# Feeding two open sums one K tile at a time, with three other groups of work moved by one to three steps, in a fused hash-attention and SiLU feed-forward kernel

## The chip, the cores and the metric

The kernel runs on one core of a Trainium2 chip. The metric is device time in microseconds (us) of one execution. Every execution quoted here is with a granted TensorE clock of 0.999 or 1.0. Engine names are those of the profile: PE is TensorE (PEld its weight loads), DVE is VectorE, ACT is ScalarE, POOL is GpSimd, SP is SyncE.

## The reference

Attention over 4 batches x 8 heads with 768 positions and head dimension 64, in which a query sees only keys with the same 6-bit hash, and then a feed-forward layer on the result.

```python
def _attn_ref(q, k, v, proj):                     # cut
    q_bits = (einsum('bhsd,dk->bhsk', q, proj) > 0)
    k_bits = (einsum('bhsd,dk->bhsk', k, proj) > 0)
    ...                                           # buckets from the bits
    mask = q_bucket[:, :, :, None] == k_bucket[:, :, None, :]
    scores = where(mask, scale * matmul(q, k.transpose(0, 1, 3, 2)), -1e9)
    ...                                           # softmax
    return matmul(attn, v)

def _moe_ref(x, w_in, w_out):                     # x: 3072 x 512, w_in: 512 x 2048
    h = x @ w_in
    g = h * (1.0 / (1.0 + exp(-h)))
    return g @ w_out
```

## The kernel before

The attention of 32 heads is cut into 288 steps, nine to a head. A step `w` multiplies the probabilities of step `w` with V (four matmuls, line 398), and then issues the score of step `w + 3` (line 366), whose exponential (line 369) runs on ACT. All other work is planned into steps as filler: transposes of Q and K, the hash projection, and the feed-forward layer of the batch before.

```python
    LEAD = 3
    ...
    for w in range(NW):
        flush()                       # products g = (th + 1) * h of the step before, on DVE
        for fn in at.pop(w, []):      # work planned into this step
            fn()
        ...
        for _ in range(n):
            moeq.popleft()()          # units of the feed-forward layer
        av(w)
        if w + LEAD < NW:
            score(w + LEAD)
```

In the timelines shown here, an engine's instructions stand in the order in which the program issues them (in step 93 of the changed kernel the projection at 65.72 us, then line 398 at 67.15 and line 366 at 67.29). The feed-forward layer of batch 0 needs the output of all four pairs of heads as its four K tiles (`xT[0]` to `xT[3]`; a K tile is one quarter of the dimension that the sum runs over). The last one exists only after step 71. So two of its sums are opened before, with the first three tiles, and left open in PSUM, the memory in which PE adds up. They share the tag `m`, which has three buffers, with the transposes and the projections.

```python
        def mm1(ci, grp, dts=slice(0, NDT)):
            ...
            hp = opened.pop((ci, grp), None)
            if hp is None:
                hp = ps.tile([P, f, n], F32, tag="m", name="h_ps", bufs=3)
            for j in range(f):
                ft = grp * f + j
                for dt in range(dts.start, dts.stop):
                    nc.tensor.matmul(hp[:, j, :], w_in16[:, dt, ft * P : (ft + 1) * P],
                                     xT[4 * b + dt][:, c0 : c0 + n],
                                     start=(dt == 0), stop=(dt == NDT - 1))
            if dts.stop < NDT:
                opened[ci, grp] = hp
                return
            th = thp.tile([P, f, n], F32, tag="th", name="th")
            nc.scalar.activation(out=th, in_=hp, func=AF.Tanh, scale=0.5)
            after.append(lambda: nc.vector.scalar_tensor_tensor(...))     # g, line 470
```

The hash bits come from a projection on PE (line 281), a comparison on DVE (line 287), and copies into the operands of the scores. For pairs up to 7 these copies are DVE instructions (lines 340 and 343), eight for two pairs; for later pairs they are DMAs:

```python
        if p > 7:
            ...
            for n in range(2):
                nc.sync.dma_start(...)
            return
        for n in range(2):
            ...                       # tensor_copy or tensor_scalar on DVE
```

The softmax here doesn't subtract the row's maximum and nothing guards it: scores larger than these inputs give would overflow.

## Time and profile before

| | before |
|---|---|
| median of the first 3 executions | 304.34 us (304.14 to 304.92) |
| span of the profiled execution | 302.8 us |
| PE / ACT / DVE / POOL busy | 98% / 69% / 60% / 42% |
| chain that ended last | PE 91%, DVE 6%, ACT 1% |

How to read it: PE looks like the limit with 98%, and for the last three quarters of the span it is. The prediction shows the views of the first quarter, where other engines set the pace. Two more lines belong to it, from the timeline of PE. The columns are start and length in us, engine, line, operation, and in brackets the idle time of PE before it and what ended that.

```profile
66.66 1.02 PE L461 MATMUL h_ps<-xT,win 128*128 128x512 f16 x4 [0.62 <-DVE g L470]
...
74.50 1.02 PE L461 MATMUL h_ps<-xT,win 128*128 128x512 f16 x4 [0.21 <-DVE g L470]
```

These are the only two waits of PE on DVE in the whole span that the page counts (0.8 us). Both are for a PSUM buffer of tag `m` that a product of line 470 must free. The first stands right after the projection of pairs 6 and 7; the change is aimed at it.

### The profile page before, as it was taken

The page shows a single profiled execution, that of the slowest core. Times are in us where ns is not written, and L with a number is a line of the kernel's source. Part 1 is how long each engine was busy: PE and PEld are TensorE (multiplying, and loading weights), DVE is VectorE, ACT ScalarE, POOL GpSimd, SP SyncE. Part 2 cuts the span into 40 slices and gives each one's busy share as a digit, 9 for nine tenths or more (in the row PEclk, how much of TensorE's full clock was granted, in tenths as well). Part 3 has the DMA queues.
Part 4 walks back from the last instruction along what each step waited for, and adds up shares of the span by engine and source line. Part 5 has one row for each costly group of instructions (what it writes and reads, how often), then busy time and mean ns, then how long its engine had stood idle before and what let it go on. Part 6 is the DMA issues. An engine that isn't in the chain of part 4 may idle for free.

```text
span 302.8 us, 7181 instructions
## 1 busy us (share of the span) xinstructions
PE 297.2 (98%) x2710; PEld 175.1 (58%) x2710; DVE 180.3 (60%) x344; ACT 210.2 (69%) x392; POOL 128.3 (42%) x203
## 2 busy tenths in 40 slices
PE   8999999999999999999999999999999999999996
PEld 3675855545665665555565665555566654446653
DVE  5797848899668454854695434854543442764332
ACT  5987989979887686878886766878877732452300
POOL 7589999286617561845149411765111100000000
PEclk9999999999999999999999999999999999999999
DMA  7999997979988737844068226011022003001112
GB/s 195 246 251 196 187 164 123 244 124 163 160 180 137 116 106 194 132 92 134 3 125 131 62 61 202 1 42 31 2 61 63 6 32 95 35 2 69 37 66 73
DMA packets 103170, 32.87 MB, mean 109 GB/s; under 512 B 90656, under 2 KB 100192, under 8 KB 103136
## 3 DMA queue, kind: packets, MB, share of 16 engines
q1 hardware_dynamic: 98752, 28.22, 44.1%
q0 software_dynamic: 4224, 4.19, 9.0%
q8 instruction: 21, 0.34, 0.5%
q14 instruction: 13, 0.11, 0.1%
q10 hardware_dynamic: 160, 0.00, 0.0%
HBM read 27.27 MB, written 6.29 MB: 111 GB/s over the span
## 4 chain that ended last, share of the span: by engine, by line
PE 91%; DVE 6%; ACT 1%; issue 1%; POOL 0%; DVEq 0%; ACTq 0%; POOLq 0%
PE o_ps L496 26%; PE h_ps L461 24%; PE s_ps L366 19%; PE o_ps L398 12%; PE bp_ps L281 3%; DVE g L470 2%; PE tp_ps L185 2%; PE warm_ps L125 1%; PE o_ps L482 1%; ACT u L369 1%; DVE qk L246 1%; PE tp_ps L198 1%; DVE qka L343 1%; PE bp_ps L225 1%; PE o_ps L389 0%
## 5 line engine op out<-in xcount | busy, mean ns | idle before, releaser
L369 ACT ACTIVATE u<-s_ps 128x512 f16<-128x512 f32 x288 | 157.1, 602 | 37.7 <-PE s_ps L366 37.2
L470 DVE SCALAR_TENSOR_TENSOR g<-th,h_ps 128x512 f16<-128x512 f32 x96 | 65.7, 689 | 75.0 <-ACT th L468 75.0
L461 PE MATMUL h_ps<-xT,win 128*128 128x512 f16 (+1 forms) x512 | 97.7, 325 | 0.8 <-DVE g L470 0.8
L398 PEld LDWEIGHTS <-u 128*128 128x128 f16 x1152 | 68.1, 98 | 41.8 <-ACT u L369 8.2
L496 PE MATMUL o_ps<-wout,g 128*128 128x512 f16 x368 | 91.6, 379 | 0.0
L468 ACT ACTIVATE th<-h_ps 128x512 f32<-128x512 f32 x96 | 58.0, 604 | 38.0 <-PE h_ps L461 35.5
L398 PE MATMUL o_ps<-vv,u 128*128 128x65 f16 x1152 | 82.6, 194 | 0.7 <-ACT u L369 0.4
L461 PEld LDWEIGHTS <-win 128*128 128x128 f16 x512 | 49.8, 98 | 32.3 <-issue 1.6
L418 POOL TENSOR_TENSOR x_pr<-osum,rec 128x384 f16<-128x384 f32 x23 | 19.0, 826 | 89.7 <-DVE rec L417 89.2
L496 PEld LDWEIGHTS <-g 128*128 128x128 f16 x368 | 35.8, 98 | 33.6
L366 PE MATMUL s_ps<-qka 71*128 71x512 f16 x192 | 52.6, 327 | 0.1
L366 PE MATMUL s_ps<-qkb 128*128 128x512 f16 x192 | 52.5, 326 | 0.0
L251 POOL TENSOR_SCALAR qka<-qk 64x1536 f16<-64x1536 f32 x15 | 22.0, 1466 | 11.5 <-DVE qk L246 6.5
L501 DVE TENSOR_SCALAR osb<-o_ps 128x512 f32<-128x512 f32 x23 | 15.8, 688 | 15.0 <-PE o_ps L496 15.0
L251 POOL TENSOR_SCALAR qkb<-qk 64x1536 f16<-64x1536 f32 x15 | 22.1, 1471 | 1.2
L262 POOL TENSOR_TENSOR vsa<-v_sb 128x192 f32<-128x192 f32 x32 | 18.9, 592 | 0.0
L260 POOL CAST vv<-v_sb 128x384 f16<-128x384 f32 x32 | 16.2, 507 | 1.8 <-DMA v_sb<-in_v_dram 1.4
L246 DVE STREAM_TRANSPOSE qk<-k_blk 128x768 f32<-128x768 f32 x10 | 15.9, 1589 | 0.3 <-issue 0.3
L246 DVE STREAM_TRANSPOSE qk<-q_blk 128x768 f32<-128x768 f32 x10 | 15.9, 1594 | 0.0
L366 PEld LDWEIGHTS <-qka 71*128 71x128 f16 x192 | 15.5, 97 | 0.7 <-ACT qka L238 0.6
L366 PEld LDWEIGHTS <-qkb 128*128 128x128 f16 x192 | 15.4, 97 | 0.0
L412 DVE TENSOR_TENSOR osum<-o_ps,vsum 128x390 f32<-128x390 f32 x23 | 13.0, 565 | 2.3
(70 smaller groups left out, 162.9 us busy)
## 6 DMA issues: line engine op xcount, KB each, us to landing
out_dram<-osb SPq DMA_DIRECT2D x23, 256.0 KB
v_sb<-in_v_dram SPq DMA_DIRECT2D x15, 384.0 KB
q_blk<-in_q_dram SPq DMA_DIRECT2D x40, 96.0 KB
k_blk<-in_k_dram SPq DMA_DIRECT2D x40, 96.0 KB
win<-in_moe_w_in_dram POOLq DMA_DIRECT2D x4, 512.0 KB, 8.0
wout<-in_moe_w_out_dram POOLq DMA_DIRECT2D x4, 512.0 KB, 6.3
q_sb<-in_q_dram SPq DMA_DIRECT2D x5, 384.0 KB
k_sb<-in_k_dram SPq DMA_DIRECT2D x5, 384.0 KB
```

The source lines that it names most:

```text
L246: nc.vector.transpose(out=dst, in_=qk_sb[p, "qk"[n]])
L251: nc.gpsimd.tensor_scalar(out=dst[rows, :], in0=qk32[p][rows, :], scalar1=CS, scalar2=1.0, op0=ALU.mult, op1=ALU.mult)
L260: nc.gpsimd.tensor_copy(out=vv[:, :, 0:D], in_=src)
L262: nc.gpsimd.tensor_tensor(out=sa, in0=src[:, 0:3], in1=src[:, 3:6], op=ALU.add)
L366: nc.tensor.matmul(sp[:, o0 : o0 + n], t[rows, S + jt * P : S + (jt + 1) * P], t[rows, c0 : c0 + n], start=True, stop=True)
L369: nc.scalar.activation(out=u, in_=sp, func=AF.Exp, scale=ESC)
L398: nc.tensor.matmul(o_ps[h][:, c0 // P + i, :], u[:, o0 + i * P : o0 + (i + 1) * P], vv[:, jt, :], start=(not direct(h) and w % NU == 0 and ...
L418: (nc.vector if direct(h) else nc.gpsimd).tensor_tensor(out=x_pr[p][:, :, par * D : (par + 1) * D], in0=o[:, 0:NJ, 0:D], in1=rec[:, :, Non ...
L461: nc.tensor.matmul(hp[:, j, :], w_in16[:, dt, ft * P : (ft + 1) * P], xT[4 * b + dt][:, c0 : c0 + n], start=(dt == 0), stop=(dt == NDT - 1))
L468: nc.scalar.activation(out=th, in_=hp, func=AF.Tanh, scale=0.5)
L470: after.append(lambda: nc.vector.scalar_tensor_tensor(out=g[ci][:, grp * f : (grp + 1) * f, :], in0=th, scalar=1.0, in1=hp, op0=ALU.add, o ...
L496: nc.tensor.matmul(o2[tt], g[ci][:, ft, ct * P : (ct + 1) * P], w_out16[:, ft, :], start=(ft == 0), stop=(ft == NFT - 1))
```

## The change

The intent is to fill PE more evenly in the early part of the program and to take the projection away from the sum that follows it. Four things move and nothing is added or removed. The two open sums get one K tile at a time, at steps 65, 67, ... 75, where before they got three tiles each at steps 66 and 70. The transposes of head 7's output, which make the fourth tile, move from step 74 to 75. The transposes and casts of pairs 4 and 5 come three steps sooner. The projection of pairs 6 and 7 comes one step later.

```diff
             hp = opened.pop((ci, grp), None)
-            if hp is None:
+            if dts.start == 0:
                 hp = ps.tile([P, f, n], F32, tag="m", name="h_ps", bufs=3)
...
-            head = slice(0, NDT - 1)
-            first = [lambda grp=grp: mm1(0, grp, head) for grp in range(2)] + \
-                [lambda grp=grp: mm1(0, grp, slice(NDT - 1, NDT)) for grp in range(2)] + first[2:]
+            one = [[lambda grp=grp, dt=dt: mm1(0, grp, slice(dt, dt + 1)) for grp in range(2)]
+                   for dt in range(NDT)]
+            first = one[0] + one[1] + one[2] + one[3] + first[2:]
...
-        plan(QST + 3 * i, lambda i=i: t_unit(4 + i // 3, i % 3))
+        plan(QST - 3 + 3 * i, lambda i=i: t_unit(4 + i // 3, i % 3))
...
-                plan(QST + 3 * i, lambda p=4 + i // 3, par=par: cast_unit(p, par))
+                plan(QST - 3 + 3 * i, lambda p=4 + i // 3, par=par: cast_unit(p, par))
...
-        wp = w0 + (24 if Q == 2 else 20)
+        wp = w0 + {2: 24, 3: 21}.get(Q, 20)
...
-        plan((30, 42, 58)[p] if p < 3 else 2 * NU * (p + 1) + (2 if p % 4 == 3 else 9),
+        plan((30, 42, 58, 75)[p] if p < 4 else 2 * NU * (p + 1) + (2 if p % 4 == 3 else 9),
...
-    for i in range(2):
-        plan(66 + 4 * i, first_units[0].pop(0))
+    for i in range(6):
+        plan(65 + 2 * i, first_units[0].pop(0))
```

## The prediction

> **What bounds the kernel now.** I read the page's totals and chain first, then busy time by stretch, then the three engines' timelines in the stretches that the change touches.
>
> ```profile
> PE 91%; DVE 6%; ACT 1%; issue 1%; POOL 0%; DVEq 0%; ACTq 0%; POOLq 0%
> ...
> L369 ACT ACTIVATE u<-s_ps 128x512 f16<-128x512 f32 x288 | 157.1, 602 | 37.7 <-PE s_ps L366 37.2
> ...
> L461 PE MATMUL h_ps<-xT,win 128*128 128x512 f16 (+1 forms) x512 | 97.7, 325 | 0.8 <-DVE g L470 0.8
> ```
>
> The chain is almost all PE, and PE waits little. But a busy PE may still be slow, so I cut the span where the program changes character (columns: us, then busy us of PE, PE weight load, DVE, ACT, POOL).
>
> ```profile
> 44.40:56.00 11.60, 11.06 (x135) 6.43 (x132) 9.57 (x17) 10.64 (x22) 8.21 (x18) 1.00 0.87 172
> 56.00:74.50 18.50, 17.67 (x168) 9.66 (x166) 18.06 (x30) 16.11 (x33) 13.12 (x17) 1.00 1.00 154
> 74.50:245.00 170.50, 170.43 (x1629) 102.73 (x1629) 96.25 (x160) 130.82 (x243) 70.41 (x109) 1.00 0.45 93
> ```
>
> Three regimes follow one another: before 56 us ACT is nearly full, from 56 to 74.5 us DVE is (18.06 of 18.50), after that PE is without a gap. Everything the change moves lies before about 77 us. After 74.5 us PE runs its queue with no wait worth counting, so whatever PE gains up to there comes out at the end one for one, and nothing else does.
>
> To place the change I counted steps: every step of the main loop leaves one group of four probability-times-V matmuls (L398), and the score of three steps later follows it. Step 0's group starts at 9.07 us; step 36 is at 31.12, step 60 at 44.39, step 66 at 47.62, step 74 at 51.91, step 92 at 67.52.
>
> The ACT timeline of steps 63 to 80, with the idle time before a run of exponentials in brackets:
>
> ```profile
> 48.22 2.06 ACT L369 ACTIVATE u<-s_ps 128x512 f16<-128x512 f32 x4 [0.18 <-PE s_ps L366]
> 50.47 3.61 ACT L369 ACTIVATE u<-s_ps 128x512 f16<-128x512 f32 x7 [0.19 <-PE s_ps L366]
> 53.95 0.62 ACT L468 ACTIVATE th<-h_ps 128x512 f32<-128x512 f32 x1
> ```
>
> The two gaps are the two heads of the open sums (steps 66 and 70). Six exponentials take 3.04 us, so queued ones start (3.04 - 0.60)/5 = 0.49, or nearer 0.48, apart, less than their length of 0.60. A bare step costs PE 0.34 us (for example 47.62 to 47.96). Hence before step 80 a step lasts 0.48 us unless PE adds more than it can hide.
>
> The DVE timeline decides a second point, when the last attention output needed for batch 0 exists:
>
> ```profile
> 44.10 1.26 DVE L287 TENSOR_SCALAR bits<-bp_ps,sc 128x512 f16<-128x512 f32 x2 [1.16 <-PE bp_ps L281]
> ...
> 50.95 0.56 DVE L418 TENSOR_TENSOR x_pr<-o_ps,rec 128x384 f16<-128x384 f32 x1
> 52.11 0.56 DVE L431 COPY xT<-xt_ps 128x768 f16<-128x768 f16 x1 [0.60 <-PE xt_ps L430]
> ```
>
> From the bits of pairs 4 and 5 (44.10) to head 7's output (50.95 + 0.56 = 51.51) DVE never stops; PE's transposes of that output start at 51.56, right behind it.
>
> Last, pieces of the chain of waits in order of time:
>
> ```profile
> 55.55 0.50 ACT th L468
> 56.07 0.69 DVE g L470
> ...
> 66.04 0.57 DVE g L470
> 66.60 1.19 DVE bits L287 x2
> ...
> 73.76 0.70 DVE g L470
> 74.50 1.02 PE h_ps L461 x4
> ```
>
> It runs on DVE from 56.07, released by the second tanh of batch 0, to 74.50, where a PE sum waits for the buffer that this DVE result frees. In between PE loses 0.62 us at 66.66 and 0.21 us at 74.50, both waiting for L470 (all of the 0.8 in the page's row).
>
> **What the Trainium skill says.** "PSUM — Partial Sum Buffer", section "The four PSUM rules": a matmul without the first flag adds where an earlier one has written, and the clearing by a first one reaches its own bank. So a sum in its own bank may stay open while other banks are used; the kernel before already does this with three of four K tiles, and the change only splits it further. "TensorE: Matmul & The Clock Gate", section "Back-to-back issue gap": N/2.4 + 2.5 ns, 216 ns at N = 512; here the three head matmuls take PE 0.65 us (49.22 to 49.87), so the trace agrees, and splitting costs nothing extra (steps 77 and 79, which already carry one such matmul, take 0.56 = 0.34 + 0.22). "ScalarE: Activation LUTs", section "What ACT_TABLE_LOAD costs": 186 + 0.833 N ns, 612 at 512, with 93 ns overlapped; the trace has 602 and a spacing of about 480, so the overlap here is larger and I use the trace. "Perfetto Trace Analysis", section "Optimization Strategy", speaks of regimes with different limiting engines; the stretches above are a case.
>
> **The change part by part.** No work is added or removed; the same instructions are issued at other steps. I carry two start times from step to step, with constants from the trace: an exponential starts 0.48 after the one before it, or 0.60 after the PE group that its scores follow (47.62 to 48.22), whichever is later; a PE group starts 0.34 plus the extra PE work after the one before it, or 0.65 after its own exponential (39.87 to 40.52), whichever is later. A tanh takes a place of 0.48 in ACT's queue. Started at step 31 this account gives the kernel before within 0.2 us up to step 90, so I trust it for differences.
>
> *Transposes sooner.* Six units of 0.44 us (four transposes; 0.78 - 0.34 at step 39) go from steps 36..51 to 33..48. With one such unit every third step PE needs (3 x 0.34 + 0.44)/3 = 0.49 per step, as much as ACT. Moving the whole comb only exchanges an empty stretch before it for one after it. The account gives -0.06 us from step 54 on.
>
> *Sums fed one K tile at a time.* Before, steps 66 and 70 carry 0.65 us each: the exponentials of steps 69 and 73 start 0.82 and 0.80 after their forerunners instead of 0.48, a loss of 0.34 + 0.32 = 0.66. After, steps 65, 67, .. 75 carry 0.22 us each: two steps need 0.34 + 0.56 = 0.90 of PE against 0.96 of ACT, and the exponential three steps on has about 0.2 us to spare. So 0.63 to 0.66 is saved by step 73. But step 75 now has transposes (0.35) and a tile (0.22) together, and PE arrives there at about 51.26 us while head 7's output, at the end of the DVE run, exists only at 51.51 - 0.06 = 51.45. PE starts the transposes at about 51.50, group 75 at 51.50 + 0.35 + 0.22 = 52.07, the exponential of step 78 at 52.67 against 53.00 before. So about half is given back: -0.33 us, the shift of the projection's start included. The two tanh follow in ACT's queue, and the DVE run from 56.07 starts 0.33 sooner.
>
> *Projection one step later.* Before, step 92 has the projection (0.34 + 1.5 us with the step) and then a sum that wants the buffer of the sum just before; hence the wait of 0.62. After, that sum comes first and takes an older buffer, and step 93 had no sum, so the wait at 66.66 goes. But DVE does the same work in another order: L470 for that sum before the bits, and all eight copies of bits (steps 93 to 96) still before the L470 (flushed at step 97) on which PE waits at 74.50. DVE had no idle time there to recover. PE arrives 0.62 sooner and waits 0.62 longer. I give this part 0.0, at most 0.07 from two small gaps (DVE 0.10 at 74.69, PE 0.07 at 76.10), and put in 0.05.
>
> Sum: -0.33 - 0.05 = -0.38. 304.34 - 0.38 = 303.96.
>
> **The rivals.** (1) *Head 7's output does not hold PE up.* Then the account alone gives -0.56 at step 80, with the last 0.05 about 303.7. For it: PE's wait in the trace before is below 0.1. Against: DVE is continuous up to that output, and nothing in the change shortens that run. (2) *The removed 0.62 us wait reaches the end*: -0.33 - 0.62, or 303.4. For it: it is the longest wait of PE after 40 us. Against: DVE busy 18.06 of 18.50. (3) *Nothing arrives*: if DVE, not ACT, set its own start at 56 us, the time stays at 304.3. Against: DVE idles 0.78 us just before 56.07, waiting for the tanh. (4) *A new wait*: two open sums hold two of the three m buffers from step 67 instead of 70; only the step 75 transposes want the third, so I see no loss.
>
> **Range and chances.** The three runs before spread over 0.8 us. Rival 2 sets the low side, rival 3 with noise the high one: 303.3 to 304.5. 2% is 6 us. Steps 31 to 81 take 28.1 us (28.20 to 56.33), 50 x 0.34 of it bare steps and some 8.3 other PE work, which leaves 2.8 to win there and 0.8 after it; both outer chances are 0.01.
>
> **What would show it.** Right: the gaps of ACT before the exponentials of steps 69 and 73 are gone; a PE wait on L418's output of about 0.2 to 0.3 us appears before the L430 transposes of step 75; the first L470 of the long DVE run comes near 55.7; the wait of PE on L470 after the projection vanishes and the one now at 74.50 grows to 0.8 or 0.9. Wrong: that last wait stays near 0.2 (then rival 2), or the span falls by over 0.7 us, or by nothing.

## The result, and the profile after

The changed kernel took 304.39 us (median of 4, 303.95 to 304.45), the kernel before 304.38 us (median of 4) in the same rounds. The ratio of times was 0.9995, with a 95% interval of 0.9978 to 1.0012. A ratio here is the mean time of one kernel's fast runs over that of the other's of the same rounds, so it is not quite the ratio of the medians quoted. By the times alone, nothing can be seen.

The profiles show more, if they are laid over each other at the right point. The PE timeline of the first microseconds differs although both programs are the same there. Kernel before:

```profile
3.27 0.87 PE L198 MATMUL tp_ps<-ident,q_row 128*128 128x128 f32 x3
...
5.52 0.85 PE L225 MATMUL bp_ps<-qk,pw 128*32 128x384 f32 x8
...
9.07 0.30 PE L398 MATMUL o_ps<-vv,u 128*128 128x65 f16 x4
```

Changed kernel:

```profile
3.41 0.87 PE L198 MATMUL tp_ps<-ident,q_row 128*128 128x128 f32 x3
...
5.71 0.97 PE L225 MATMUL bp_ps<-qk,pw 128*32 128x384 f32 x8
...
9.38 0.30 PE L398 MATMUL o_ps<-vv,u 128*128 128x65 f16 x4
```

The first transposes began 0.14 us later here, and the first projection took 0.97 us where it took 0.85 (its successor began at 6.61 and not at 6.30), so step 0 began at 9.38 and not at 9.07 us. These 0.31 us stay in every start time that follows, and they cover up the gain of the change. To see that gain I use a distance: from the start of step 30's group of line 398 to the start of step 104's. Step 30 lies before everything that was moved (27.63 us before, 27.93 after), and step 104 after it (77.35 and 77.22). The distance is 49.72 us before and 49.29 us after: 0.43 us were won. From step 104 to step 287 both profiles take 167.77 us, so nothing is won or lost there.

The stretches of the changed kernel, with the columns of the prediction's view:

```profile
44.40:56.00 11.60, 11.20 (x139) 6.38 (x132) 9.79 (x17) 10.50 (x22) 8.55 (x19) 1.00 0.93 137
56.00:74.50 18.50, 17.66 (x169) 9.68 (x167) 18.08 (x30) 16.93 (x34) 13.12 (x17) 1.00 1.08 192
```

DVE is as full between 56 and 74.5 us as it was (18.08 for 18.06 us).

ACT's timeline of steps 65 to 78:

```profile
46.20 6.48 ACT L369 ACTIVATE u<-s_ps 128x512 f16<-128x512 f32 x13
52.96 0.60 ACT L369 ACTIVATE u<-s_ps 128x512 f16<-128x512 f32 x1 [0.27 <-PE s_ps L366]
```

Thirteen exponentials now run without a gap; the two gaps of 0.18 and 0.19 us are gone. But there is a new one of 0.27 us at 52.96. PE's timeline shows where it comes from:

```profile
51.27 0.30 PE L398 MATMUL o_ps<-vv,u 128*128 128x65 f16 x4
51.40 0.38 PE L366 MATMUL s_ps<-qka 71*128 71x512 f16 x1
51.80 0.51 PE L430 MATMUL xt_ps<-ident,x_pr 128*128 128x128 f16 x6
```

Two 512-column matmuls in sequence start 0.22 us apart elsewhere in this trace (52.14 and 52.36, for example). The transposes of line 430 could have started at 51.62 and started at 51.80: PE stood 0.18 us behind head 7's output, which DVE finished at 51.74. (No bracket appears there, since the modelled end of the score lies at 51.78.) The rest of the gap of 0.27 comes from the transposes and the tile in one step: in e7 below, where PE does not wait there, a gap of 0.08 us is left.

Further on, PE's timeline has one wait on DVE in place of two:

```profile
64.43 1.02 PE L461 MATMUL h_ps<-xT,win 128*128 128x512 f16 x4
...
65.72 1.50 PE L281 MATMUL bp_ps<-qk,pw 128*32 128x512 f32 x16
...
74.38 1.02 PE L461 MATMUL h_ps<-xT,win 128*128 128x512 f16 x4 [0.84 <-DVE g L470]
```

The sum now comes ahead of the projection and waits for nothing. The wait of 0.62 us is gone, and the wait that was 0.21 us at 74.50 is 0.84 at 74.38. Their sum was 0.83 and is 0.84. The bracket counts from the modelled end of the score before it. The expectations below count by the length of step 101, which is 1.58 us before, 2.21 in the changed kernel and 1.21 in e5, where PE does not wait: 0.37 and 1.00 us. By either count this wait grew by 0.63.

DVE's timeline of the changed kernel shows why. The sum at 74.38 needs the buffer of the last product here, which ends at 73.64 + 0.69 = 74.33, behind the copies of bits and without a gap of more than 0.03 us:

```profile
69.97 0.60 DVE L340 TENSOR_SCALAR qkb<-bits,sc 13x768 f16<-13x768 f16 x1
70.60 0.69 DVE L470 SCALAR_TENSOR_TENSOR g<-th,h_ps 128x512 f16<-128x512 f32 x1
71.32 1.10 DVE L343 COPY qka<-bits 13x768 f16<-13x768 f16 x2
72.44 0.54 DVE L343 COPY qkb<-bits 13x768 f16<-13x768 f16 x1
73.00 0.61 DVE L340 TENSOR_SCALAR qkb<-bits,sc 13x768 f16<-13x768 f16 x1
73.64 0.69 DVE L470 SCALAR_TENSOR_TENSOR g<-th,h_ps 128x512 f16<-128x512 f32 x1
```

The chain of the changed kernel shows 2% on a DMA of V, ahead of a line 470 product at 59 us that does not read V. I take that for a wrong guess of the releaser: DVE runs through there as it did before.

### The profile page after: what moved, and what is told of

Same layout as the page of the kernel before. It is cut to its first block, busy times and chain, and to the rows that moved or that the text cites. A ratio compares the mean times of both kernels' runs of the same rounds, so it can differ in the third digit from the quotient of the medians.

```text
span 302.6 us, 7181 instructions
## 1 busy us (share of the span) xinstructions
PE 297.0 (98%) x2710; PEld 175.1 (58%) x2710; DVE 180.0 (59%) x344; ACT 210.1 (69%) x392; POOL 128.2 (42%) x203
## 4 chain that ended last, share of the span: by engine, by line
PE 89%; DVE 5%; DMA 2%; issue 1%; SPq 1%; ACT 1%; POOL 0%; DVEq 0%; ACTq 0%; POOLq 0%
PE o_ps L496 26%; PE h_ps L461 24%; PE s_ps L366 18%; PE o_ps L398 11%; PE bp_ps L281 3%; DMA v_sb<-in_v_dram 2%; PE tp_ps L185 2%; DVE g L470 2%; PE o_ps L482 1%; PE warm_ps L125 1%; SPq L92 1%; DVE qka L343 1%; PE bp_ps L225 1%; DVE qk L246 1%; PE tp_ps L198 0%
```

## The experiments

Ten runs were made, each of five rounds against the kernel before, all correct (e4 is the changed kernel again, e10 is e5 again). "Distance" is the one from step 30 to step 104.

| run | distance, us | step 30 starts at | median (range) of 6, us | ratio, 95% interval |
|---|---|---|---|---|
| before (profile) | 49.72 | 27.63 | | |
| changed (profile) | 49.29 | 27.93 | | 0.9995 (0.9978 to 1.0012) |
| e1 transposes only | 49.60 | 27.58 | 304.38 (304.17 to 305.19) | 0.9991 (0.9971 to 1.0011) |
| e2 tiles only | 49.38 | 27.87 | 304.18 (304.04 to 304.43) | 0.9980 (0.9964 to 0.9995) |
| e3 projection only | 49.67 | 27.73 | 304.67 (304.11 to 305.18) | 0.9995 (0.9978 to 1.0012) |
| e4 changed again | 49.29 | 28.12 | 304.47 (303.88 to 304.91) | 0.9986 (0.9969 to 1.0003) |
| e5 changed, bits 6, 7 by DMA | 48.20 | 27.58 | 303.69 (302.95 to 305.69) | 0.9979 (0.9952 to 1.0006) |
| e6 same without the projection's move | 48.78 | 27.63 | 303.65 (303.46 to 304.26) | 0.9969 (0.9955 to 0.9982) |
| e7 changed, bits 5, 6, 7 by DMA | 48.03 | 27.71 | 303.45 (302.81 to 304.70) | 0.9971 (0.9949 to 0.9993) |
| e8 before, bits 6, 7 by DMA | 49.21 | 27.56 | 304.34 (303.80 to 304.82) | 0.9989 (0.9973 to 1.0004) |
| e9 as e7, transposes at step 74 | 47.94 | 27.64 | 303.56 (303.01 to 303.98) | 0.9956 (0.9942 to 0.9971) |
| e10 = e5 again | 48.22 | 27.59 | 303.26 (302.95 to 304.68) | 0.9959 (0.9939 to 0.9979) |

The kernel before ran 11 times beside each group of runs: 305.14 us median for e1 to e4, 304.51 for e5 to e8, 304.74 for e9 and e10. Each group ran on another chip, so times are compared within a group only. The theory is the prediction's: DVE, full from 56 us on, takes back what the projection's move gives. The rival is that a wait taken away from PE is time won.

### One part at a time: e1, e2, e3, and the whole again: e4

e1 holds the two lines of the diff with `QST - 3`, e2 the open sums and the step 75 transposes, e3 the single line `wp = w0 + {2: 24, 3: 21}.get(Q, 20)`; e4 is the changed kernel unedited.

> Only the transposes and casts of pairs 4 and 5 are three steps sooner. Yardstick for all runs: from the start of step 30's group of four L398 matmuls to the start of step 104's, which leaves out the first microseconds; it is 49.72 us in the kernel before (27.63 to 77.35) and 49.29 in the changed one (27.93 to 77.22). Theory (moving a comb of equal units inside an ACT-bound stretch only exchanges one empty stretch for another): 49.6 to 49.7. Rival (the transposes are where the gain comes from): 49.3 to 49.4. Ratio of times to before 0.999 to 1.001 for both.

Measured 49.60: won 0.12. Half of it, 0.06, is there by step 80 (27.43 us from step 30, against 27.49), and 0.06 more comes at step 92, whose group starts 3.37 after the one before it instead of 3.44 (more on this under e3). The transposes are not where the gain comes from.

> Only the open sums are fed one K tile at a time (with the transposes of head 7's output at step 75). Theory: exponentials of steps 69 and 73 start 0.48 after their forerunners, PE then waits about 0.2 us for head 7's output at step 75, and 49.35 to 49.50 remains of 49.72; the 0.62 us wait after the projection (step 92) is still there. Rival (no gain without the projection's move): 49.65 to 49.75.

Measured 49.38: won 0.34. Up to step 80 it is 0.27 (27.22 against 27.49); the other 0.07 comes at step 92, as in e1. Step 75's group starts 1.09 us after step 74's, as in the changed kernel: 0.34 for the step, 0.57 for the transposes and the tile, 0.18 of waiting. The wait after the projection is 0.57 us. This part gives most of the gain, as the theory said, and needs no help from the projection's move.

> Only the projection of pairs 6 and 7 is one step later. Theory (DVE is full from 56 us to the result that frees a buffer for PE at step 101): the wait of 0.62 us at step 92 goes, the wait at step 101 grows from 0.37 (1.58 - 1.21) to about 1.0, and the yardstick is 49.62 to 49.72. Rival (the wait removed is time won): the wait at step 101 stays below 0.4 and the yardstick falls to about 49.1.

Measured 49.67: won 0.05. PE's timeline of e3 has this wait, and none after the projection:

```profile
74.55 1.02 PE L461 MATMUL h_ps<-xT,win 128*128 128x512 f16 x4 [0.84 <-DVE g L470]
```

A wait of 0.62 us was removed at step 92 and came back at step 101, nine steps on. The rival, 49.1, is out. The three parts alone add up to 0.12 + 0.34 + 0.05 = 0.51; together they give 0.43. A part of each comes from one stretch of DVE, in which DVE has the same instructions in all these kernels. From the product of line 470 with which the long run starts (56.07 us before) to the product at 65.95 us, DVE takes 9.88 us in the kernel before, 9.82 in e1, 9.81 in e2, 9.84 in e3 and 9.81 in the changed kernel. Single products there last up to 0.77 us in the kernel before and at most 0.70 in e2 and the changed kernel. So 0.06, 0.07 and 0.04 of the three gains are the same 0.07 of the whole, which is about the difference. Why the lengths differ is open. The program of e3 is that of the kernel before up to step 91, so 0.04 us are a difference from profile to profile, and of the 0.05 that e3 won about 0.01 is left for the projection's move.

> The whole change once more, for its time and for the first microseconds. Theory: the yardstick repeats 49.29 within 0.05 whatever the start does; step 30's group starts at another time than 27.93 in some profiles, by up to 0.5 us, since the first matmuls run at two speeds. Ratio of times 0.998 to 1.000. Rival (the change itself delays the start): step 30's group again near 27.93 here and 27.63 in runs whose first 60 us are as in the kernel before.

The distance is 49.29 again, while step 30 starts at 28.12. Over all twelve profiles step 30 starts between 27.56 and 28.12 and without regard to what was changed behind it: e5, with all of the change, and e8, with none of it, lie at 27.58 and 27.56. In e4 PE waited for an input besides (line 198, on the DMA of the first K rows):

```profile
4.37 0.90 PE L198 MATMUL tp_ps<-ident,k_row 128*128 128x128 f32 x3 [0.22 <-DMA k_row<-in_k_dram]
```

So the change does not delay the start: e5 issues the same as the changed kernel there. The start varies by 0.56 us from profile to profile, from the landing of inputs and from the speed of the first matmuls. For the second, "TensorE: Matmul & The Clock Gate", section "What's actually happening", says that the clock is released after a busy window of about 3.4 us that runs freely and not from the kernel's start, so that the point of release varies by 500 ns either way. The profiles fit that: the two warm-up matmuls of line 125 after the first transposes start 0.43 us apart in the kernel before and in the changed one (at 4.71 and 5.14), but 0.22 apart in e5, e8 and e10 (4.69 and 4.91 in e5), and the two halves of the first projection start 0.47 us apart in the changed kernel and 0.34 in e5. No run here sets out to test it.

### Taking work off DVE: e5, e6, e8, and e10

If DVE's queue is the reason why the projection's move brings nothing, the move must be worth its 0.6 us as soon as DVE has slack. The copies of bits can go to DMA, by a path that the kernel has for later pairs; the rows that never change are already in the buffers from pairs 2 and 3.

```diff
-        if p > 7:
+        if p > 5:
```

e5 is the changed kernel with this line, e6 has `wp` as before, e8 is the kernel before with this line alone.

> The changed kernel, with the eight copies of bits of pairs 6 and 7 taken off DVE (about 4.5 us of its work between 67.8 and 73.7 us) and given to DMA, as later pairs have it. Theory (DVE's order of work sets PE's wait at step 101): the result that PE waits for is there some 4 us sooner, the wait of 1.00 us at step 101 goes, and the yardstick from step 30 to step 104 falls from 49.29 to about 48.2 to 48.4, the time to a ratio of 0.994 to 0.997 of the kernel before. Rival (the wait comes from ACT or from the order of buffers): 49.2 to 49.3 as before.

Measured 48.20, which is 1.09 below the changed kernel. The forecast of the ratio was missed: it is 0.9979, with an interval that holds 1 (e10, the same kernel again, has 0.9959). The waits of PE from 40 us to the end, in the view of waits (total us, times, longest):

```profile
PE o_ps L398 <- ACT u L369: 0.4, 1, 0.4
```

No wait on line 470 is left. DVE's timeline now has gaps in the stretch in which it had none:

```profile
66.65 1.26 DVE L287 TENSOR_SCALAR bits<-bp_ps,sc 128x512 f16<-128x512 f32 x2
68.83 0.69 DVE L470 SCALAR_TENSOR_TENSOR g<-th,h_ps 128x512 f16<-128x512 f32 x1 [0.93 <-ACT th L468]
70.42 0.69 DVE L470 SCALAR_TENSOR_TENSOR g<-th,h_ps 128x512 f16<-128x512 f32 x1 [0.90 <-ACT th L468]
```

> As the run before it, but the projection stays at step 92. Theory (the projection's move is worth its 0.62 us once DVE has slack): the wait of 0.62 us at step 92 is back, none at step 101, yardstick 48.8 to 49.0, about 0.6 above the run with the move. Rival (the move is worth nothing in any case): within 0.1 of the run with the move.

Measured 48.78 (0.02 under the range expected), with the wait back at its old place:

```profile
66.22 1.02 PE L461 MATMUL h_ps<-xT,win 128*128 128x512 f16 x4 [0.56 <-DVE g L470]
```

The projection's move is worth 48.78 - 48.20 = 0.58 us here, and at most 49.72 - 49.67 = 0.05 us where DVE is full. That is the answer to the question where its 0.6 us went. The rival of e6 (no difference) is out as well.

> The kernel before with the eight copies of bits of pairs 6 and 7 by DMA, nothing else. Theory: the wait of 0.62 us at step 92 stays, the one of 0.37 at step 101 and the 0.06 at step 103 go, yardstick 49.2 to 49.35 (49.72 before). Rival (DVE's copies do not matter): 49.7.

Measured 49.21, 0.51 below the kernel before: the waits of steps 101 and 103 are gone and the one of step 92 remains (0.6 us in the view of waits). By this distance the line alone brings a little more than the whole change (0.43).

The six times of e5 spread over 2.7 us, which its profile (of an execution of 302.95 us) does not explain.

> The kernel of e5 once more, whose six times spread over 2.7 us (302.95 to 305.69) where its profile shows nothing slow. Theory (the spread is from execution to execution and not of this kernel): the yardstick is 48.20 within 0.05 again, the profile of a slow execution, if one is caught, differs before step 30 or in the output after step 287, and the median lies between 302.9 and 304.0. Rival (DMA of bits comes late in some executions): a profile with a PE or ACT wait on the bits and a yardstick above 48.5.

The distance was 48.22 and the median 303.26. Five of six times lie between 302.95 and 303.79, the sixth at 304.68. The profile was again of a quick execution (302.99), so no slow one was seen from within, and where those lose their time stays open; that the DMA of bits comes late in some executions is not ruled out.

### Head 7's output: e7 and e9

e7 takes the copies of pair 5 off DVE too (`p > 4`), which shortens the DVE run ahead of head 7's output. e9 puts the transposes of that output back to step 74 in e7.

```diff
-        plan((30, 42, 58, 75)[p] if p < 4 else ...
+        plan((30, 42, 58, 74)[p] if p < 4 else ...
```

> As e5, with pair 5's four copies of bits by DMA as well, which shortens DVE's run up to head 7's output by about 2.3 us. Theory (that run makes PE wait 0.18 us at step 75): the wait there goes, step 75's group comes 0.91 after step 74's instead of 1.09, and the yardstick is 0.15 to 0.2 below e5's. Rival (something else holds step 75): 1.09 again and the same yardstick as e5.

Measured 48.03, 0.17 below e5, and step 75's group starts 0.90 after step 74's. DVE has the output done at 50.21 + 0.56 = 50.77 us and waits for PE ahead of it:

```profile
49.98 0.20 DVE L417 RECIPROCAL rec<-o_ps 128x6 f32<-128x6 f32 x1 [1.60 <-PE o_ps L398]
50.21 0.56 DVE L418 TENSOR_TENSOR x_pr<-o_ps,rec 128x384 f16<-128x384 f32 x1
```

So the wait of 0.18 us at step 75 was for head 7's output, as the theory had it.

> As e7, with the transposes of head 7's output back at step 74, which carries no tile of the open sums, so that step 75 no longer has both. Theory (head 7's output is early enough now, and one step with 0.35 and one with 0.22 us of extra PE work delay the exponentials less than one with 0.57): no wait at step 74, yardstick 47.9 to 48.05 (e7: 48.03), and the lowest time of all kernels with e7, ratio 0.993 to 0.997. Rival (the output is still late at step 74): step 74's group over 0.8 after step 73's, yardstick above 48.1.

Measured 47.94; step 74's group starts 0.68 after step 73's, which is 0.34 for the step and 0.34 for the transposes, so there is no wait. The distance is the shortest of all, 1.78 us below the kernel before and 1.35 below the changed one. Its ratio of 0.9956 has an interval clear of 1, so e9 is faster than the kernel before by some 0.4%; the intervals of e10, e6, e7 and e2 lie below 1 as well. After step 287, e7 and e9 take 57.88 and 57.87 us to the end against 57.62 to 57.64 in the other profiles. PE's matmuls start at the same times there in e7 as in e5, counted from step 287, and so does the last DMA of the output. The 0.25 us arise behind it: SyncE's closing waits (line 697) come in another order, and four of them, about 0.06 us each, which in e5 are over before the longest wait ends, follow it in e7 and e9.

## Why the prediction was right

The prediction was 303.96 us, 0.38 below the kernel before, with a range of 303.3 to 304.5; measured were 304.39 and, in the second set, 304.47 us. The range held, but it would have held without any gain too (the kernel before took 304.38 in the same rounds), and the spans fell by only 0.14 us (302.76 and 302.62 in the traces), near to the fall "by nothing" that the prediction named as a sign of being wrong. So the times say little for or against the mechanism. The 0.38 cannot be checked in the times: the intervals of the two ratios allow anything from 0.9 us faster to 0.4 us slower. It can be checked in the distances, 0.43 us in both profiles of the change: 0.35 up to step 80, and 0.08 after it.

- **Transposes sooner**, predicted -0.06 from step 54 on: e1 shows -0.06 at step 80. The other -0.06 of e1, at step 92, is the stretch of DVE described under e3, which the account did not have.
- **One tile at a time**, predicted -0.33 with the transposes' -0.06 in it: at step 80 the changed kernel is 27.14 us from step 30, against 27.49, which is -0.35. The gaps at steps 69 and 73 went, as said, and the step 75 transposes gave about half of it back. The wait there was put at 0.2 to 0.3 us and is 0.18; e7 shows that it was for head 7's output, so rival 1 is false.
- **Projection one step later**, predicted 0.0 to -0.07, with -0.05 put in: e3 gives -0.05 and the changed kernel -0.08 after step 80. That the number fits is luck. The two small gaps from which it was to come are still there in e3 (DVE's 0.10 us ahead of line 412, and step 103 with 1.31 us against 1.30), and 0.04 of e3's 0.05, as 0.07 of the 0.08, is the stretch of DVE described under e3. That the move itself brings next to nothing was right, and so was its reason. The wait on line 470 was to grow to 0.8 or 0.9 us, and it is 0.84. e5 against e6 shows the cause; rival 2 (the 0.62 us arrives) fails on e3.
- **DVE's long run starts sooner**, near 55.7 us: it starts at 56.03 in the profile, and less the 0.31 us of the late start that is 55.72. Rival 3 (DVE sets its own start, and nothing arrives) fails on the 0.43 us.
- **A new wait for buffers**, rival 4: none was seen between steps 67 and 75 other than the one for head 7's output.

What the prediction lacked was the size of the noise beside its effect. It took the spread of three executions, 0.8 us, for the range, and then gave a middle of 0.38 us below as if a handful of executions could show it. The start of the program alone varies by 0.56 us between profiles. The first profiles, compared by their spans, would have given 0.14 us, a third of the gain.

## What to carry to other kernels

In this kernel, a wait removed from the engine that ends the program was only worth what the next engine's queue left of it. So before moving the waiter, ask whether the engine that it waited for has idle time between here and the next place where the two meet. If it has none, take work off that engine first; here one changed number did that, and made the same move worth 0.58 us instead of 0.05 at most. And when the expected gain is smaller than the spread of the times, compare profiles between two fixed points of the program, from before the first change to after the last, and profile the unchanged kernel more than once: here one stretch of the same instructions differed by 0.04 us.

## What the Trainium skill lacked or had wrong

- "ScalarE: Activation LUTs", section "What ACT_TABLE_LOAD costs": back-to-back activations are said to overlap by about 93 ns. Here a 128x512 exponential lasts about 0.60 us at the start of a queued run and the next one starts 0.47 to 0.49 us later, so they overlap by about 0.12; by the end of the changed kernel's run of thirteen one lasts 0.73 us at the same spacing, an overlap of 0.25.
- "TensorE: Matmul & The Clock Gate", section "Back-to-back issue gap": it gives about 131 ns per matmul at N = 512 for a stream with weight loads, beside 216 ns for the isolated gap. In this kernel's stream with a weight load for every matmul, the spacing is 0.22 us throughout (three in 0.65 us, at 49.22 to 49.87), so only the second figure fits.
- "Perfetto Trace Analysis", section "Optimization Strategy": it tells how to find the gap of the contended engine and what ends it, but not that a gap removed can come back whole at the next meeting with the same queue. Here 0.62 us at step 92 became 0.63 us more at step 101 (0.21 to 0.84).
